# Moving output stores and transposes in the DMA queue of a fused sparse-attention and feed-forward kernel

## The chip, the cores and the metric

The kernel runs on one core of one Trainium2 chip. The metric is the device time of one execution in microseconds (us). The kernel before takes 322.76 us, the median of three runs (322.28, 322.76 and 325.9).

## What is computed

The reference first does attention over 8 batches of 8 heads with 576 positions of 64 numbers each. The first four heads are "local": a position sees itself and the 31 positions before it. The last four are "strided": a position sees those positions up to its own that have the same remainder modulo 32. The result, 4608 tokens of 512 numbers, goes through a bilinear feed-forward layer.

```python
scores = scale * np.matmul(q, k.transpose(0, 1, 3, 2))
scores = np.where(masks[None, :, :, :], scores, -1000000000.0)
attn = np.exp(scores - np.max(scores, axis=-1, keepdims=True))
attn = attn / (np.sum(attn, axis=-1, keepdims=True) + 1e-09)
x = np.matmul(attn, v).transpose(0, 2, 1, 3).reshape(B * S, H * D)
out = (x @ w_a) * (x @ w_b) @ w_out        # 512 -> 1536 -> 512
```

## The kernel before

**The feed-forward layer sets the beat.** The 4608 tokens are worked in nine passes t = 0 to 8 of 512 tokens. A pass has 16 slots, numbered 16t to 16t + 15. Slots 0 to 11 of a pass are its twelve groups of 128 hidden channels (`ffn_ab`): matrix products with w_a and w_b (TensorE, line 621), a copy of the first to SBUF by ScalarE (642), their product by VectorE (645) into `pf`. Slots 12 to 15 are the output product with w_out. In passes 1 to 8 this uses seven products of halves in place of eight (`y_plan`, matmuls at line 890), with sums made beforehand on VectorE (`fast_s`, line 824). Parts of the output are copied or added into two buffers `y_sb` of 512 KB each by `y_post` (ScalarE 855 and 861, VectorE 853, 857, 859), in the order 1, 7, 6, 4, 5, 2, 3. Parts 1 and 7 go to the first buffer, parts 6 and 5 to the second, so the third copy at line 855 is the first write to the second buffer. There are two buffers in all, and each pass uses both again. `store_half` sends one buffer to DRAM (store 0 and store 1, line 886).

**Attention is laid between these slots.** Batches are counted from 0 in the code, so the third batch is b = 2 and the fourth b = 3. A table names steps and their places: `STEPS` for batches 1 and 2, `LATER` for batches from 3 on, which run in pass b - 1. A whole number is the end of a slot; a half, such as 23.5, is the middle of the slot after it (24), between the two matrix products. The steps that matter here:

- `S0` to `S7`: scores of one unit (TensorE 378), exponential (ScalarE 398), mask (VectorE 416). S0 to S3 are local, S4 to S7 strided.
- `V0` to `V7`: the weighted sums. For local units TensorE (459), then a reciprocal (467) and a product (485) on VectorE into `xl`. For strided units TensorE (518), a logarithm and an exponential on ScalarE (525, 526; from pass 3 on 530, 531), a product on VectorE (527; 533) straight into `xT`.
- `O0`, `O1`: rows of the local heads from `xl` to a scratch in DRAM (`rows_out`, DMA of SyncE, line 500). `I0`, `I1`: back from it, transposed, into `xT` (`rows_in`, line 505), which the feed-forward layer reads.
- `Q0` to `Q3`: copies of transposed queries into zero-padded buffers `qz` (VectorE 334). Q0 and Q1 are local, Q2 and Q3 strided; S4 to S7 read what both Q2 and Q3 wrote.

**Loads and transposes.** `load_qk` lets POOL copy keys and queries of a batch into bf16 rows in DRAM (208 and 210, tensors `kr` and `qr`); `step_D` reads them back transposed through SyncE: line 321 for local keys and local queries, 324 for strided keys, 327 for strided queries in four pieces. The buffers are `kT` (two, by the batch's parity) and `qTl`, `qTs` (one each). `load_vl` (219) and `load_vs` (237) load values through POOL. Before a slot's POOL work a one-element copy (`pace`, 1138) makes POOL wait for that slot's result, so POOL's loads follow the passes.

**Order.** The instructions of each engine run in the order in which the program emits them. SyncE (SP) emits nothing but DMAs and their waits: stores, O, I and step_D all stand in its one queue, and one that waits holds those behind it. `do(i, fn)` puts a call at the end of slot i, behind the steps of the table with that number. For batches from 4 on step_D is placed in pass b - 2.

Of the kernel before, what the change touches and what calls it, by code (L numbers as in the profile page):

```python
# [32 lines left out]
def kernel(  # L33
# [531 lines left out]
    def F_mm(f, w, kk):  # L565
# [12 lines left out]
    STEPS = {1: {5.5: "Tk2", 6: "Tq2", 7: "S4 Tk3", 7.5: "S5", 8: "Tq3", 8.5: "V4", 9: "S6 V5 Pk0", 9.5: "S7 Pq0",  # L578
                 10: "V6 Tk0", 10.5: "Tq0 Pk1", 11: "Pq1", 12: "V7 Tk1 S0 W0 W1", 12.5: "Tq1 W2",
                 12.6: "S1", 12.75: "L0 X2", 13: "s2 X3 V0 m2 L1 W3", 13.5: "V1 S3", 14: "V2 X0", 14.5: "V3", 15: "X1"},  # L580
             2: {18: "Q0 Q1", 20: "S0", 20.5: "S1", 21: "V0", 21.5: "S2 Q2", 22: "V1 Q3", 22.5: "S3 O0", 23.5: "V2",
                 24: "S4 I0", 24.5: "V3 O1", 25: "S5", 25.5: "V4", 26: "S6", 26.5: "I1", 27: "V5", 27.5: "S7", ("y", 1, 6): "V6",
                 30: "V7"}}
    LATER = {-4: "Q0", -3: "Q1", -1: "S0", 0: "S1", 1: "V0", 2: "S2 Q2", 3: "V1 O0", 4: "S3 Q3", 5: "V2", 6: "S4", 7: "V3 O1 I0", 8: "S5", 9: "V4 I1",
             10: "S6",
# [13 lines left out]
    def take(pos):  # L599
        for b, names in steps.get(pos, ()):  # L600
            run(b, names)
# [5 lines left out]
    def mm_bank(shape):  # L607
        nm = "tp" if used[0] % 4 == 3 and used[0] >= 0 else "mm"
        used[0] += 1
        return psum4[nm].tile(shape, F32, tag=nm, name="mm")  # L610
# [218 lines left out]
    def products(t):  # L829
        pf, s = pfs[t], pss[t]  # L830
        full = lambda e, i: (lambda g, q: pf[:, 2 * g + e, HT * i + q:HT * (i + 1):2])
        summed = lambda n: (lambda g, q: s[:, n, g, q:HT:2])
        wsum = lambda n: (lambda g: wf[:, n, g])
        wfull = lambda e, j: (lambda g: wov[:, e, j, g])
        return {"1": ("X", full(0, 0), wfull(0, 0)), "2": ("Y", full(1, 0), wfull(1, 0)), "3": ("X", summed(3), wfull(1, 1)),
                "4": ("Z", full(1, 1), wsum(3)), "5": ("X", summed(0), wsum(0)), "6": ("X", summed(1), wsum(1)),
                "7": ("Z", summed(2), wsum(2))}
# [8 lines left out]
    def y_bufs():  # L846
        return [fsb.tile([128, 2, d_model], F32, tag="y_sb", name="y_sb", bufs=2) for _ in range(2)]

    def y_post(k, y, q, bank, n=slice(0, HN)):

        part = lambda i, j: y[i][:, q, HN * j:HN * (j + 1)]
        if k == "+":
            nc.vector.tensor_tensor(part(1, 1), part(1, 1), part(0, 1), op=ALU.add)  # L853
        elif k in "1765":
            nc.scalar.copy({"1": part(0, 0), "7": part(0, 1), "6": part(1, 0), "5": part(1, 1)}[k], bank)  # L855
        elif k == "4":
            nc.vector.tensor_tensor(part(1, 0), bank, part(1, 0), op=ALU.add)
        elif k == "2":
            nc.vector.tensor_tensor(y[0][:, q, n], bank, y[0][:, q, n], op=ALU.add)
        elif k == "3":  # L860
            nc.scalar.copy(part(0, 1), bank)
# [4 lines left out]
    def by_block(order, lead):  # L866

        head = order[:lead]
        return [(k, q, g) for k, q in head for g in range(FG - 1)] + [(k, q, FG - 1) for k, q in head] + [
            (k, q, g) for k, q in order[lead:] for g in range(FG)]  # L870

    def bank_of(nm, shape):
        return psum4[nm].tile(shape, F32, tag=nm, name="mm")

    def y_plan(t):

        plan, y = products(t), y_bufs()
        late = t in FAST_A
        if late:
            bank = {x: bank_of(nm, [128, 2, HN]) for x, nm in (("X", "mm"), ("Z", "mm"), ("Y", "tp"))}  # L880
        else:
            bank = {x: mm_bank([128, 2, HN]) for x in "ZXY"}

        def store_half(i):
            rows = out[TTOK * t:TTOK * (t + 1)].rearrange("(a i s q) c -> a s i (q c)", i=2, s=8, q=2)
            nc.sync.dma_start(out=rows[:, :, i], in_=y[i].rearrange("p q c -> p (q c)"))

        for k, q, g in by_block(Y_ORDER, 2 if late else 0):
            b, lhs, rhs = plan[k]
            nc.tensor.matmul(bank[b][:, q], lhsT=lhs(g, q), rhs=rhs(g), start=k in "172" and q == 0 and g == 0,  # L890
                             stop=g == FG - 1, skip_group_check=True)
            if g == FG - 1:
                if q == 1:
                    y_post(k, y, slice(0, 2), bank[b])
                    if k == "5":
                        y_post("+", y, slice(0, 2), None)
                take(("y", t, Y_ORDER.index((k, q)) + 1))
            yield y
        do(16 * t + 17, store_half, 0)
        do(16 * t + 18, store_half, 1)  # L900

    def y_tail(t):

# [30 lines left out]
    def ffn_ys(t, j, mid):  # L934
        if j == 0:
            yst[t] = (y_tail if t == NT - 1 else y_plan)(t)
        for i in range(21):
            y = next(yst[t])
            if i == 10:
                mid()  # L940
        if j == 3:
            for _ in yst[t]:
                pass
        return (y[0][:1, 0, :1], None, y[1][:1, 0, HN:HN + 1], y[1][:1, 0, :1])[j]
# [36 lines left out]
    with tc.manual_schedule(engines={ENG.PE, ENG.SP, ENG.Pool, ENG.DVE, ENG.Activation}):  # L981
# [26 lines left out]
        for nm in ORDER:  # L1008
            if nm[0] == "*":
                spin(int(nm[1:]))  # L1010
            elif nm in ("Ck", "Cq"):
                n = nm[1]
                x, cp = {"k": (raw[0], nc.vector.tensor_copy), "q": (raw[1], nc.scalar.copy)}[n]
                t = nats[0, n, False][:, 0:2].rearrange("p h r d -> p (h r d)")
# [54 lines left out]
        def do(i, fn, *args):  # L1069
            at.setdefault(i, []).append(lambda: fn(*args))  # L1070
# [11 lines left out]
        for b in range(FIRST_D, B):  # L1082
            g0 = 16 * (b - 2)
            if b == FIRST_D:
                do(0, load_qk, b, False)
                do(1, load_qk, b, True)
                do(14, load_vl, b)
                for h in range(HL):
                    do((16, 18, 19, 20)[h], load_vs, b, (h,))
            else:  # L1090
                do(19 if b == FIRST_D + 1 else g0 - 2, load_qk, b, False)
                do(21 if b == FIRST_D + 1 else g0 + 2, load_qk, b, True)
                for h in range(HL):
                    do(g0 + h + (15 if b == FIRST_D + 1 else 11), load_vs, b, (h,))
                do(g0 + (12 if b == FIRST_D + 1 else 9), load_vl, b)
            gs = {2: (13, 14, 15, 15), 3: (6, 6, 8, 14)}.get(b) or (3, 3, 4, 4)
            for (z, nm), g in zip(((0, "k"), (0, "q"), (1, "k"), (1, "q")), gs):
                do(g0 + g, step_D, b, z, nm)
        for n in range(4):
# [72 lines left out]
```

## Time and profile before

| What | Value |
|---|---|
| Median of the three runs | 322.76 us |
| The profiled execution's own time | 324.58 us |
| Its span, first to last instruction | 322.8 us |
| TensorE busy | 312.6 us |
| VectorE, ScalarE, POOL busy | 250.8, 192.9, 119.2 us |
| Granted TensorE clock | 0.999 |
| Stores of 512 KB by SyncE | 14 |
| Pass 1, pass 2 begin (TensorE) | 57.1, 91.0 us |
| Output products of passes 2, 3, 4, 5 begin | 117.3, 150.6, 184.0, 217.3 us |

Times in the profile are microseconds from the span's start. In a timeline a row gives start, duration, engine, line, operation, what it writes and what it reads, shapes, how many instructions were merged, and in square brackets the engine's idle time ahead of it and what ended that. For SyncE the duration is that of the issuing instruction; the time until the data has landed is told apart from it, in the answers on a line or a tensor. A list of waits gives who waited for whom: us in total, times, longest.

### The profile page before, as it was taken

To read this page: it belongs to the slowest core of one execution; us is meant where nothing else is said; L and a number is where in the kernel's file an instruction comes from. 1 tells how busy PE (TensorE), PEld (TensorE's weight loads), DVE (VectorE), ACT (ScalarE), POOL (GpSimd) and SP (SyncE) were. 2 spreads that over 40 slices of the span, in tenths; PEclk is the share of its full clock that TensorE was granted. 3 is DMA by queue.
4 is the path that set the end of the run, shared out by engine and by line. 5 is a ranking of instruction groups with operands and counts; after the bars stand their busy time and mean duration, and the time that the engine had idled before them with its cause. 6 is when DMAs were issued, how large, how long until landed. Compare 5 with 4: busy or idle time off the path is not lost.

```text
span 322.8 us, 7276 instructions
## 1 busy us (share of the span) xinstructions
PE 312.6 (97%) x2742; PEld 215.7 (67%) x2742; DVE 250.8 (78%) x574; ACT 192.9 (60%) x374; POOL 119.2 (37%) x211
## 2 busy tenths in 40 slices
PE   7999999999969999999999999999999999999994
PEld 5754565455945578656999996659655866786684
DVE  5877876588747988899689868997899667857862
ACT  6963776456744476558655775567656655535541
POOL 8845702781255143514550336133201012203520
PEclk9999999999999999999999999999999999999999
DMA  8999999999699999999999999989512040004004
GB/s 149 168 205 202 204 182 225 189 100 186 100 117 249 178 75 87 177 163 142 104 150 183 125 132 139 178 131 137 141 21 55 2 126 6 1 3 131 0 2 130
DMA packets 127059, 40.31 MB, mean 125 GB/s; under 512 B 114864, under 2 KB 124144, under 8 KB 126832
## 3 DMA queue, kind: packets, MB, share of 16 engines
q0 software_dynamic: 79760, 19.20, 63.6%
q1 hardware_dynamic: 47120, 20.59, 34.5%
q8 instruction: 21, 0.34, 0.5%
q14 instruction: 14, 0.11, 0.1%
q10 hardware_dynamic: 144, 0.07, 0.1%
HBM read 38.93 MB, written 18.28 MB: 177 GB/s over the span
## 4 chain that ended last, share of the span: by engine, by line
PE 90%; DMA 4%; DVE 3%; issue 1%; ACT 1%; POOL 0%; POOLq 0%
PE mm L621 36%; PE mm L890 17%; PE mm L770 6%; PE mm L706 4%; PE st L378 4%; PE mm L952 3%; PE ax L763 3%; PE o L459 3%; PE mm L763 2%; PE e L692 2%; DMA xT<-xd 2%; DMA shared<-in_q_dram 2%; PE mm L917 2%; PE mm L692 2%; PE end L917 1%; PE o L518 1%
## 5 line engine op out<-in xcount | busy, mean ns | idle before, releaser
L621 PE MATMUL mm<-xT,wa_sb 128*128 128x512 bf16 (+1 forms) x304 | 72.1, 356 | 2.6 <-DMA xT<-xd 2.6
L621 PE MATMUL mm<-xT,wb_sb 128*128 128x512 bf16 (+1 forms) x304 | 72.0, 357 | 0.0
L642 ACT COPY a_sb<-mm 128x512 f32<-128x512 f32 x68 | 39.8, 586 | 33.1 <-PE mm L621 31.4
L1138 POOL CAST pace<-pf 1x1 f32<-1x1 bf16 x71 | 20.8, 293 | 91.6 <-DVE pf L645 52.7
L645 DVE TENSOR_TENSOR pf<-a_sb,mm 128x512 bf16<-128x512 f32 x58 | 39.4, 679 | 12.2 <-ACT a_sb L642 8.6
L621 PEld LDWEIGHTS <-wb_sb 128*128 128x128 bf16 x304 | 29.2, 98 | 29.3 <-issue 2.9
L398 ACT ACTIVATE p<-st 72x576 bf16<-72x576 f32 (+1 forms) x56 | 36.4, 650 | 14.2 <-PE st L378 13.6
L621 PEld LDWEIGHTS <-wa_sb 128*128 128x128 bf16 x304 | 27.3, 98 | 17.4
L890 PEld LDWEIGHTS <-ps 128*128 128x128 bf16 x336 | 32.7, 98 | 3.7
L890 PE MATMUL mm<-wf,ps 128*128 128x256 bf16 x252 | 29.8, 273 | 0.0
L855 ACT COPY y_sb<-mm 128x512 f32<-128x512 f32 (+1 forms) x32 | 17.9, 559 | 19.1 <-PE mm L890 14.9
L1138 POOL COPY pace<-y_sb 1x1 f32<-1x1 f32 x22 | 9.7, 439 | 53.2 <-DVE y_sb L853 27.2
L770 PE MATMUL mm<-xT,wb_sb 128*128 128x512 bf16 x88 | 26.2, 379 | 0.0
L890 PEld LDWEIGHTS <-pf 128*128 128x128 bf16 x252 | 23.5, 98 | 2.7
L237 POOL DMA_DIRECT2D vs<-in_v_dram x24 | 21.8, 909 | 4.6 <-issue 3.1
L890 PE MATMUL mm<-wo_sb,pf 128*128 128x256 bf16 x168 | 21.8, 273 | 0.0
L824 DVE TENSOR_TENSOR ps<-pf 128x512 bf16<-128x512 bf16 (+1 forms) x49 | 19.6, 400 | 0.8
L706 PE MATMUL mm<-xT,wb_sb 128*128 128x512 bf16 (+1 forms) x80 | 19.1, 336 | 0.0
L416 DVE TENSOR_TENSOR p<-p,mask_l 128x576 int16<-128x576 int16 x32 | 14.5, 454 | 5.8 <-ACT p L398 5.5
L533 DVE TENSOR_TENSOR xT<-o,xr 64x288 bf16<-64x288 f32 x16 | 7.7, 480 | 13.5 <-ACT xr L531 13.4
L459 PEld LDWEIGHTS <-p 128*128 128x128 bf16 (+1 forms) x256 | 13.1, 97 | 6.2 <-DVE xr L485 1.0
L416 DVE TENSOR_TENSOR p<-p,mask_s 72x576 int16<-72x576 int16 x28 | 12.6, 451 | 1.9 <-ACT p L398 1.7
(211 smaller groups left out, 639.4 us busy)
## 6 DMA issues: line engine op xcount, KB each, us to landing
out_dram<-y_sb SPq DMA_DIRECT2D x14, 512.0 KB, 5.1
kr<-in_k_dram POOLq DMA_DIRECT2D x12, 288.0 KB, 8.5
qr<-in_q_dram POOLq DMA_DIRECT2D x12, 288.0 KB, 9.3
vl<-in_v_dram POOLq DMA_DIRECT2D x6, 384.0 KB, 7.2
out_dram<-y_sb SPq DMA_DIRECT2D x7, 256.0 KB, 3.3
vs<-in_v_dram POOLq DMA_DIRECT2D x24, 72.0 KB, 4.9
xd<-xl SPq DMA_DIRECT2D x12, 144.0 KB, 4.3
wo_sb<-in_moe_w_out_dram POOLq DMA_DIRECT2D x4, 384.0 KB, 11.3
```

The costliest lines, as they stand in the source:

```text
L237: nc.gpsimd.dma_start(out=vs_buf[b % 2][:, h, :, 0:D], in_=v[b, HL + h].rearrange("(p r) d -> p r d", r=RS))
L398: nc.scalar.activation(p_flat(p)[:M, :2 * W].rearrange("p (i n) -> p i n", n=2 * n), st[:M].rearrange("p a (i n) -> p (a i) n", n=256)[:, ...
L416: nc.vector.tensor_tensor(pi, pi, mk, op=ALU.bitwise_and)
L459: nc.tensor.matmul(of[:, j, i, :w], lhsT=pt, rhs=vt, start=True, stop=True)
L621: nc.tensor.matmul(ps_[:, c0:c0 + n], lhsT=w[:, kk, 128 * f:128 * (f + 1)], rhs=xT[:, kk, x0:x0 + n], start=(kk == first and c0 == 0), sto ...
L642: nc.scalar.copy(a_sb, ab[0])
L645: nc.vector.tensor_mul(pf[:, f, :].rearrange("p (i a s) -> p a i s", i=2, s=16), halves(a_sb), halves(ab[1]))
L706: nc.tensor.matmul(dst, lhsT=wb_sb[:, kk, 128 * f:128 * (f + 1)], rhs=rhs, start=kk == 0 and k in (None, 0), stop=kk == KD - 1 and k in (N ...
L770: nc.tensor.matmul(got[e], lhsT=wb_sb[:, kk, 128 * f:128 * (f + 1)], rhs=xT[:, kk, x0:x0 + TTOK], start=kk == 0, stop=kk == KD - 1)
L824: nc.vector.tensor_tensor(s[:, n], a, b, op=op)
L890: nc.tensor.matmul(bank[b][:, q], lhsT=lhs(g, q), rhs=rhs(g), start=k in "172" and q == 0 and g == 0, stop=g == FG - 1, skip_group_check=True)
L1138: nc.gpsimd.tensor_copy(pace, done)
```

## The change

Three things move; no operation is added or taken away, but for POOL's one-element pace copies, which stand only in slots that have such a call.

1. In pass 1, the table of batch 2 (the third batch): V2 goes from the middle of slot 24 to the end of slot 23, S4 from the end of slot 24 to its middle, V3 and O1 from the middle of slot 25 to the end of slot 24, S5 from the end of slot 25 to its middle. I0 stays at the end of slot 24, now ahead of O1. Q3 goes from the end of slot 22 to the end of slot 23.
2. Batch 3 (the fourth batch): the transpose of its strided keys goes from slot 24 to slot 30, that of its strided queries from slot 30 to slot 31. For batches 4 to 7 the transpose of the local keys goes from group 3 to group 2 of its pass, ahead of O0.
3. The two stores of a pass go from groups 1 and 2 of the next pass to groups 3 and 7. In group 3 store 0 stands behind O0 and the local queries' transpose; in group 7 store 1 stands behind O1 and I0.

```diff
-             2: {18: "Q0 Q1", 20: "S0", 20.5: "S1", 21: "V0", 21.5: "S2 Q2", 22: "V1 Q3", 22.5: "S3 O0", 23.5: "V2",
-                 24: "S4 I0", 24.5: "V3 O1", 25: "S5", 25.5: "V4", 26: "S6", 26.5: "I1", 27: "V5", 27.5: "S7", ("y", 1, 6): "V6",
+             2: {18: "Q0 Q1", 20: "S0", 20.5: "S1", 21: "V0", 21.5: "S2 Q2", 22: "V1", 22.5: "S3 O0", 23: "V2 Q3",
+                 23.5: "S4", 24: "V3 I0 O1", 24.5: "S5", 25.5: "V4", 26: "S6", 26.5: "I1", 27: "V5", 27.5: "S7", ("y", 1, 6): "V6",
                  30: "V7"}}
...
-        do(16 * t + 17, store_half, 0)
-        do(16 * t + 18, store_half, 1)
+        do(16 * t + 19, store_half, 0)
+        do(16 * t + 23, store_half, 1)
...
-            gs = {2: (13, 14, 15, 15), 3: (6, 6, 8, 14)}.get(b) or (3, 3, 4, 4)
+            gs = {2: (13, 14, 15, 15), 3: (6, 6, 14, 15)}.get(b) or (2, 3, 4, 4)
             for (z, nm), g in zip(((0, "k"), (0, "q"), (1, "k"), (1, "q")), gs):
                 do(g0 + g, step_D, b, z, nm)
```

The SyncE queue of pass 4, as an example, in the new order: local keys (321), O0, local queries (321), store 0, strided keys (324), strided queries (327, four), O1, I0, store 1, I1. In the old order: store 0, store 1, O0, local keys, local queries, strided keys, strided queries, O1, I0, I1.

## The prediction

> **What bounds the kernel now.** First the page's busy times and clock: TensorE works 97% of the span at full clock. Then the waits, those of TensorE alone: after the start-up only one is worth anything.
>
> ```profile
> PE 312.6 (97%) x2742; PEld 215.7 (67%) x2742; DVE 250.8 (78%) x574; ACT 192.9 (60%) x374; POOL 119.2 (37%) x211
> PEclk9999999999999999999999999999999999999999
> ...
> PE mm L621 <- DMA xT<-xd: 2.6, 1, 2.6
> ```
>
> So no edit to queues can win more than those 2.64 us, 0.8% of the span, and any new wait of TensorE adds in full, since it has no other idle time to absorb it. The chain that ended last shows where the wait comes from, at the turn from pass 1 to pass 2:
>
> ```profile
> 85.48 3.62 DMA xd<-xl
> 89.11 5.54 DMA xT<-xd
> 94.69 1.02 PE mm L621 x4
> ```
>
> Rows of the third batch go out to DRAM (O1, 85.48), come back transposed (I1, 89.11), and TensorE, ready at 94.69 - 2.64 = 92.05, starts at 94.69. Next the timeline of SyncE, which issues one after the other:
>
> ```profile
> 78.44 0.53 SPq L500 DMA_DIRECT2D xd<-xl  x1
> 82.82 1.16 SPq L505 DMA_TRANSPOSE xT<-xd  x1
> 84.08 1.31 SPq L324 DMA_TRANSPOSE kT1s<-kr  x1
> 85.48 0.53 SPq L500 DMA_DIRECT2D xd<-xl  x1
> ```
>
> O1 stands behind the fourth batch's strided key transpose (L324). Its data was done long before: the last xl of VectorE (L485) runs 76.67 to 77.22.
>
> **Part 1: pass 1, third and fourth batch.** The L324 transpose leaves this place, so O1 follows I0 at 84.1, 1.4 us sooner. It landed 3.6 us after its issue, behind L324; with a quiet queue (237.8, 245.3) 2.2 to 2.7. I take 2.9: landed at 87.0, where I1 is issued. I1 took 5.5 us beside a load of vl (issued 84.51, landing 7.7 us later), I0 at 82.82 without one 2.6: it lands at 89.6 to 92.5, against 94.7.
>
> The same edit puts Q3 (L334, a copy into qz) one group later, to the end of group 7 (slot 23), and its reader S4 (TensorE, L378) half a slot sooner, to the middle of slot 24. VectorE runs behind TensorE there:
>
> ```profile
> 72.32 0.46 DVE L334 COPY qz0s<-qTs 64x1152 bf16<-64x1152 bf16 x1
> 72.81 0.43 DVE L824 TENSOR_TENSOR ps<-ps,pf 128x512 bf16<-128x512 bf16 x1
> 73.16 0.45 DVE L416 TENSOR_TENSOR p<-p,mask_l 128x576 int16<-128x576 int16 x1
> 73.52 0.68 DVE L645 TENSOR_TENSOR pf<-a_sb,mm 128x512 bf16<-128x512 f32 x1
> ...
> 73.02 0.35 PE L459 MATMUL o<-vl,p 128*128 128x65 bf16 x6
> 74.06 0.41 PE L378 MATMUL st<-qz0s,kT0s 128*128 128x144 bf16 x4
> ```
>
> VectorE's new order is L824, mask, pf, then V2's reciprocal (0.18) and product (0.55), then Q3 (0.46). Without Q3 at 72.32 pf ends near 73.6; plus 0.18, 0.55, 0.46 and gaps, Q3 ends at 74.85. S4's turn comes where V2 stood, 73.02, plus 0.35 for V2 now ahead of it and its wait for V1's product (72.29): 73.35. TensorE waits some **1.5 us**; behind S4 stand the second half of group 8, V3, S5 and ScalarE's exponential, on which VectorE's mask waits in turn, so all of pass 1 goes 1.6 us later. At worst S4 waits for the whole DVE lag, 2.6; at best (VectorE taking its work in the gaps) nothing. TensorE then wants its rows at 92.05 + 1.6 = 93.65; I1, even with vl shifted the same 1.6, has landed. Gain: 94.69 - 93.65 = **1.0 us**, between 0 and 2.64.
>
> Fourth batch's transposes: the four of queries (L327, 5.86 us of SyncE, from 90.33) now follow I1 and L324: 87.0 + 1.1 + 1.3 = 89.5, no later than before. Their first reader is VectorE's copy at 100.94, just after they land (100.8); its reader S4 runs at 107.20. Cost 0; if they came 3 us late, S4 has six to spare. It is the strided keys' first reader as well.
>
> **Part 2: passes 2 to 5, the stores.** In SyncE's queue store 0 moves behind the local query transpose, store 1 behind O1 and I0, the local key transpose ahead of O0. What changes is when store 1 lands, because its buffer (y_sb, two buffers) is written again by the same pass's third output copy on ScalarE (L855). This timeline row shows that the copy does wait for SyncE's DMAs:
>
> ```profile
> 154.99 0.59 ACT L855 COPY y_sb<-mm 128x512 f32<-128x512 f32 x1 [0.77 <-DMA qTs<-qr]
> ```
>
> The releaser named shares its semaphore with the old store, landed at 137.4; there TensorE ended that idle time. Behind the copy TensorE accumulates into the bank that it reads (156.32 in pass 3): slack 156.32 - 155.58 = 0.7; through V6's logarithm, exponential and product to V7 about 0.5. Every further us is one of TensorE.
>
> Store 1's issue, from pass 4's rows:
>
> ```profile
> 171.09 0.33 SPq L500 DMA_DIRECT2D xd<-xl  x1
> 171.70 2.78 SPq L321 DMA_TRANSPOSE kT0l<-kr  x1
> 174.68 2.88 SPq L321 DMA_TRANSPOSE qTl<-qr  x1
> 177.66 1.30 SPq L324 DMA_TRANSPOSE kT0s<-kr  x1
> 179.06 5.90 SPq L327 DMA_TRANSPOSE qTs<-qr  x4
> 185.05 0.53 SPq L500 DMA_DIRECT2D xd<-xl  x1
> 185.63 4.84 SPq L505 DMA_TRANSPOSE xT<-xd  x2
> ```
>
> O0 waits for V1 and stays. After it: L321 of queries 2.9, store 0 0.6, L324 1.3, four L327 5.0 to 5.9, O1 0.5, I0 1.2, gaps 0.5: 12.0 to 12.9 us. Store 1 is issued at 183.5 to 184.4; from the O0 of passes 2, 3, 5 (103.17, 137.77, 204.51) likewise 115.5, 150.2, 216.9 at the earliest. A store of 512 KB landed 4.1 us after issue where nothing else ran (261.8), 4.6 to 5.9 as first of a pair beside loads, 6.4 to 9.1 as second. The copies start at 121.7, 155.0, 188.5, 221.7.
> - Lower bound: 4.1 gives landings at 119.6, 154.3, 187.6, 221.0, all in time: cost 0. It can't go below that, since TensorE waits for no load or store in these passes now.
> - Upper bound: landings on this queue come in the order of issue, so store 1 lands behind I0. I0 landed at 123.6, 158.2, 190.9, 224.0 (5.9, 5.0, 5.3, 5.2 after issue), held up by the vl load (L219, at 114.7, 148.2, 181.6, 215.2, landing 6.5 to 7.4 later). If I0 does not come sooner, store 1 adds the 0.6 to 1.25 by which the second of a quiet pair lands behind the first: waits of up to 3.1, 4.4, 3.7, 3.5, less four slacks of 0.5: 12.7.
> - Between: 6.0 us, just over the first stores of the busy pairs. Landings 121.5, 156.2, 189.5, 222.9; waits 0, 1.2, 1.0, 1.2, less slack: **1.9 us**. I take this, because SyncE issues the transposes 1 to 2 us sooner and more of them are through before vl's packets come.
>
> One row decides how far to trust that: the last L327 of pass 4, issued 183.7, lands 5.4 us later, 189.1, just after vl (181.6 + 7.1 = 188.7). SyncE's transposes starve while POOL's load runs. The Trainium skill, "DMA: Bandwidth & Descriptors", section "Queues, rings and completion order", says that each engine takes turns between the queue rows that have work, packet by packet. By that, store 1 would get its turn beside vl; the row speaks against it for transposes, and no run here shows it for 4 KB pieces.
>
> The key transpose ahead of O0 delays O0 only if its rows are late. They landed 10.4 to 10.6 us after issue beside the stores (128.3, 161.2, 194.7), 5.6 and 6.6 without (66.6, 90.5). At 6.6 L321 is over by 137.4, 170.7, 204.1, just ahead of O0: cost 0; at 10.4 O0 and store 1 come 3 us later and the upper bound holds. I1 in pass 3 landed at 160.7 against a need at 161.64: SyncE's lead of 1 to 2 us covers the store now ahead of it. One pace copy less per pass on POOL (63% idle): 0.
>
> **Passes 6 to 8:** 0. In pass 6 store 1 follows I0 at 247, eight us before its copy (255.0); later passes hold no transposes.
>
> **Sum:** -1.0 + 1.9 = **+0.9 us**, on the profiled execution's own 324.58 (span 322.8 and 1.8 around it) 325.5. The median of the runs shown, 322.76, lies 1.8 below that execution: **323.7**. A measurement tells about 1% (3.2 us) from no change.
>
> **Rivals and chances.**
> - Forecast, some of both: 322.3 to 326, 0.38.
> - Store 1 gets its turn beside vl and lands in time; only part 1 counts: 322.76 - 1.0 = 321.8. For: lone stores take 4.1. Against: five transposes stand ahead of it. This is the outcome by that rule of the Trainium skill. 0.20.
> - No wait for Q3 either: 322.76 - 2.64 = 320.1. For it VectorE must not lag; its rows show 1.4 us. 0.07.
> - Slower: store 1 waits behind I0 and vl. With I0 1.2 us sooner and the store 1.2 behind it, it lands at 123.6, 158.2, 190.9, 224.0: waits 1.9, 3.2, 2.4, 2.3, less 2.4 of slack, 7.4; minus 1.0 gives **329.2**. It decides from landings of some 6.8 us on. For: the starved L327. 0.30.
> - The change misses its aim: I1 falls into the shifted vl load, the row wait stays beside the new ones: 322.76 + 1.9 = 324.7. 0.05.
>
> Range: 320.0 to 330.0 takes in all but the ends. Faster by over 1% (under 319.5) needs more than the one wait holds: 0.04. Slower by over 1% (over 326.0): the fourth case, 0.30. Within: 0.66.
>
> **What would show it.** TensorE's wait for xT gone; a wait of TensorE or its weight load for VectorE at S4 of 1 to 2 us near 73; O1 right behind I0. In passes 2 to 5, ScalarE's idle time ahead of the third L855 over 0.8 and ended by a DMA, TensorE waiting for ScalarE right after. I am wrong if these copies start on time and S4 too (then 320), or if key rows still take 10 us (then near 330).

## The result, and the profile after

The changed kernel is slower. Its median is 338.23 us of five runs (335.73 to 341.62), that of the kernel before 324.62 us of five (322.28 to 329.33; the three runs told above and two more). The ratio is 1.0415, with a 95% interval of 1.0317 to 1.0513; it leaves out single disturbed executions, and so it is not just the quotient of the medians. The forecast was 323.7 us with a range up to 330.0: both are missed, on the slow side.

The profiled execution after took 335.73 us, its span is 334.0 us, 11.2 us above the span before (322.8). First the page's busy times and clock, as before the change:

```profile
PE 315.3 (94%) x2714; PEld 217.7 (65%) x2742; DVE 251.8 (75%) x574; ACT 192.9 (58%) x374; POOL 117.4 (35%) x207
PEclk9999999999999999999999979999899999999999
```

TensorE is busy for 2.7 us more than before, with the same work (28 of its 2742 products are missing from this trace), and two slices of its clock row are no longer full. Next, TensorE's waits (in total, times, longest):

```profile
PE mm L890 <- ACT y_sb L855: 8.2, 4, 2.3
PE st L378 <- DVE qz0s L334: 1.3, 1, 1.3
```

The wait for `xT` is gone. Four waits of the output products for ScalarE's third copy have come in its place, one in each of the passes 2 to 5, and one wait of S4 for Q3's copy. ScalarE's own list says what that copy waits for:

```profile
ACT y_sb L855 <- DMA out_dram<-y_sb: 14.7, 4, 4.0
```

That is store 1, all four times: the copy starts 0.1 us after store 1 has landed in each of these passes. In pass 4 the timeline shows the chain. ScalarE is idle for 3.96 us ahead of the copy (0.77 us before the change), and TensorE for 2.33 us ahead of its next products in that bank.

```profile
194.48 0.59 ACT L855 COPY y_sb<-mm 128x512 f32<-128x512 f32 x1 [3.96 <-DMA out_dram<-y_sb]
195.12 2.02 PE L890 MATMUL mm<-wf,ps 128*128 128x256 bf16 x12 [2.33 <-ACT y_sb L855]
```

After two of the four waits TensorE goes on at half speed for a while. The answer on windows gives, for each stretch, its length, TensorE's busy time with the number of instructions, the granted clock, the share of the DMA engines (above 1 where transfers queue, since one counts in the stretch in which it starts) and GB/s:

```profile
192.00:195.90 3.90, 1.57 (x16) 1.00 1.31 204
195.90:199.30 3.40, 3.40 (x24) 0.50 0.07 7
199.30:202.70 3.40, 3.35 (x26) 1.00 0.38 27
233.40:236.80 3.40, 3.40 (x24) 0.50 0.04 8
```

The two half-speed stretches last 3.41 us each and do 1.7 us of work, so each costs 1.7 us.

Where the 11.2 us of the span are, stage by stage (us from one stage's first product to the next's):

| Stage | Before | After | Difference |
|---|---|---|---|
| Start-up | 22.4 | 21.4 | -1.0 |
| Pass 0 and the channel groups of pass 1 | 58.4 | 60.0 | +1.6 |
| Pass 2, channel groups | 26.3 | 23.9 | -2.4 |
| Output products of passes 2, 3, 4, 5 | 10.2 each | 12.4, 12.6, 14.3, 14.0 | +12.5 |
| All the rest | | | +0.5 |

The 12.5 us of the output products are the four waits (1.80, 2.01, 2.33, 2.02: 8.2), the two half-speed stretches (3.4), and some 0.9 that is left, most of it in passes 2 and 3, where V7 starts 0.4 us later than the wait alone makes it. The start-up differs between executions of one kernel: in three executions of the kernel before, the output products of pass 1 begin at 79.7, 80.0 and 80.8 us.

### The profile page after: what moved, and what is told of

The parts are those of the page before. It is cut to its first block, busy times and chain, and to the rows that moved or that the text cites. A ratio compares the mean times of both kernels' runs of the same rounds, so it can differ in the third digit from the quotient of the medians.

```text
span 334.0 us, 7236 instructions
## 1 busy us (share of the span) xinstructions
PE 315.3 (94%) x2714; PEld 217.7 (65%) x2742; DVE 251.8 (75%) x574; ACT 192.9 (58%) x374; POOL 117.4 (35%) x207
## 5 line engine op out<-in xcount | busy, mean ns | idle before, releaser
L621 PE MATMUL mm<-xT,wa_sb 128*128 128x512 bf16 (+1 forms) x287 | 70.3, 355 | 0.6
L1138 POOL CAST pace<-pf 1x1 f32<-1x1 bf16 x68 | 19.6, 288 | 91.1 <-DVE pf L645 44.3
L890 PE MATMUL mm<-wf,ps 128*128 128x256 bf16 x252 | 30.5, 276 | 8.2 <-ACT y_sb L855 8.2
L890 PEld LDWEIGHTS <-pf 128*128 128x128 bf16 x252 | 24.6, 102 | 3.6
L770 PE MATMUL mm<-xT,wb_sb 128*128 128x512 bf16 x83 | 25.2, 379 | 0.1
L890 PE MATMUL mm<-wo_sb,pf 128*128 128x256 bf16 x168 | 24.1, 291 | 0.0
L416 DVE TENSOR_TENSOR p<-p,mask_l 128x576 int16<-128x576 int16 x32 | 14.5, 454 | 6.4 <-ACT p L398 6.0
L459 PEld LDWEIGHTS <-p 128*128 128x128 bf16 (+1 forms) x256 | 13.2, 97 | 6.7 <-DVE xr L485 1.0
L416 DVE TENSOR_TENSOR p<-p,mask_s 72x576 int16<-72x576 int16 x28 | 12.6, 451 | 2.7 <-ACT p L398 2.5
```

The source lines that it names most:

```text
L416: nc.vector.tensor_tensor(pi, pi, mk, op=ALU.bitwise_and)
L621: nc.tensor.matmul(ps_[:, c0:c0 + n], lhsT=w[:, kk, 128 * f:128 * (f + 1)], rhs=xT[:, kk, x0:x0 + n], start=(kk == first and c0 == 0), sto ...
L770: nc.tensor.matmul(got[e], lhsT=wb_sb[:, kk, 128 * f:128 * (f + 1)], rhs=xT[:, kk, x0:x0 + TTOK], start=kk == 0, stop=kk == KD - 1)
L1138: nc.gpsimd.tensor_copy(pace, done)
```

## The experiments

The questions were: which of the parts costs the time; whether store 1 is late because SyncE issues it late (store 0 now stands ahead of the strided key transpose) or because its landing is held by POOL's `vl` load (theory C in the expectations); and what part 1 is worth alone. Each ratio is against the kernel before on the same chip.

**The two stores alone.** Edit to the kernel before:

```diff
-        do(16 * t + 17, store_half, 0)
-        do(16 * t + 18, store_half, 1)
+        do(16 * t + 19, store_half, 0)
+        do(16 * t + 23, store_half, 1)
```

> The two stores alone in groups 3 and 7; everything else as before. Theory A: the third output copy waits in passes 2 to 5 as in the changed kernel (ScalarE idle 3 to 4 us ahead of it, TensorE 2 us each); 8 to 13 us slower than before, and the wait for xT stays. Rival (it takes the key transpose ahead of O0 as well, which pushes all of SyncE's queue back): under 5 us slower.

Measured: 341.72 us, ratio 1.0580 (1.0520 to 1.0639). It is the whole loss and more: some 19 us where 8 to 13 were expected, with the expected waits, but three of them twice as long. TensorE's waits for the third copy are 4.75, 2.02, 4.04 and 3.78 us, and the clock row shows three slow places:

```profile
PE mm L890 <- ACT y_sb L855: 14.6, 4, 4.7
PE mm L621 <- DMA xT<-xd: 0.7, 1, 0.7
...
PEclk9999999999999978999999989999899999999999
```

So the other moves of the change make the stores cheaper, not dearer.

**The changed kernel with its stores back.** Edit to the changed kernel: the same four lines the other way.

> The changed kernel with both stores back in groups 1 and 2: part 1 and the key transposes in group 2 remain. If the stores are the whole loss, it is like the part 1 kernel: within 1% of before, no wait of the third copy, the S4 wait of 1.3 us. If the key transpose ahead of O0 costs something of its own, it is 1% or more slower than before and TensorE shows a wait other than S4's.

Measured: 322.88 us (10 runs), ratio 1.0017 (0.9984 to 1.0051), no wait for the third copy. With the run above this settles the first question: the stores are the loss.

**Store 1 alone.** Edit to the kernel before: only `16 * t + 18` to `16 * t + 23` for store 1.

> The kernel before with store 1 alone moved, to group 7. If store 1's place behind O1 and I0 is enough, the third copy waits in passes 2 to 5 here too, TensorE 1.5 us or more each, and this kernel is 7 us or more slower than before. If it takes both stores, the waits are under 0.7 us and the time is within 3 us of before.

Measured: 334.32 us, ratio 1.0352 (1.0280 to 1.0425); waits of 1.61, 1.56, 1.75 and 2.29 us, and one half-speed stretch behind the last. As the first case expected, store 1 in group 7 is enough for most of the loss, with store 0 left where it was.

**Store 0 back in group 1.** Edit to the changed kernel:

```diff
-        do(16 * t + 19, store_half, 0)
+        do(16 * t + 17, store_half, 0)
```

> The changed kernel with store 0 back in group 1 and store 1 left in group 7. If store 0 among the transposes is what makes SyncE's strided key transpose take 2.7 to 3.5 us in place of 1.3 to 2.6, store 1 is issued 1.5 to 2.5 us sooner after O0 (12.5 to 13.5 us in place of 14.5 to 15.3) and TensorE's waits fall to 0 to 0.8 us each: 6 to 12 us under the changed kernel. If the number of transposes in flight sets it, the waits stay at 1.5 us or more.

Measured: 332.93 us, ratio 1.0287 (1.0229 to 1.0345). SyncE's timeline of pass 4, first of the changed kernel, then of this one:

```profile
173.97 2.12 SPq L500 DMA_DIRECT2D xd<-xl  x1
176.19 1.56 SPq L321 DMA_TRANSPOSE qTl<-qr  x1
177.85 0.58 SPq L886 DMA_DIRECT2D out_dram<-y_sb  x1
178.52 3.00 SPq L324 DMA_TRANSPOSE kT0s<-kr  x1
181.62 5.68 SPq L327 DMA_TRANSPOSE qTs<-qr  x4
187.39 0.53 SPq L500 DMA_DIRECT2D xd<-xl  x1
187.97 1.25 SPq L505 DMA_TRANSPOSE xT<-xd  x1
189.27 0.59 SPq L886 DMA_DIRECT2D out_dram<-y_sb  x1
```

```profile
177.91 1.49 SPq L324 DMA_TRANSPOSE kT0s<-kr  x1
179.51 5.80 SPq L327 DMA_TRANSPOSE qTs<-qr  x4
185.41 0.53 SPq L500 DMA_DIRECT2D xd<-xl  x1
185.99 1.28 SPq L505 DMA_TRANSPOSE xT<-xd  x1
187.31 0.60 SPq L886 DMA_DIRECT2D out_dram<-y_sb  x1
```

The strided key transpose takes SyncE 1.25 to 1.99 us in the four passes here, 2.73 to 3.50 with store 0 just ahead of it. But the waits hardly change, where the first case expected 0 to 0.8 us, and there is no half-speed stretch:

```profile
PE mm L890 <- ACT y_sb L855: 7.9, 4, 2.2
```

Counted from the first output product of its pass, store 1 is now issued 0.4 to 1.4 us behind it (before this edit 1.0 to 2.6), and lands 7.0 to 7.35 us behind it (7.0 to 7.5). A store that is issued sooner and lands at the same time must be held by something else; the next two runs ask whether that is the `vl` load.

**Without the vl load.** Batches 4 to 7 get no `vl` load, first in the changed kernel:

```diff
-                do(g0 + (12 if b == FIRST_D + 1 else 9), load_vl, b)
+                if b == FIRST_D + 1:
+                    do(g0 + 12, load_vl, b)
```

> The changed kernel with the load of local values (line 219) left out for batches 4 to 7, whose local heads then use the values of older batches; nothing else is left out. Theory C (O1, I0 and store 1 stand still while POOL's load of vl runs and land only behind it, 4.3 to 5.1 us after the output products begin): without it O1 and I0 land 2.5 to 4 us after their issue, store 1 some 4.1 to 4.7 after its own, that is 5.2 to 7 us after the output products begin in place of 7.0 to 7.5; TensorE's waits fall from 8.2 us in all to 2 to 4. Rival (SyncE's late issue of store 1 alone): landing 4.6 to 5.9 us after issue as before, waits unchanged.

Measured in a single execution: 340.94 us. The waits are 0.16, 4.43, 1.81 and 4.97 us, 11.4 in all, where theory C expected 2 to 4. O1 landed 2.6 to 3.0 us after its issue, as it expected, and so did I0 in three of the four passes (2.7 to 3.6); store 1 took 4.5 to 5.8 us, where 4.1 to 4.7 were expected. But store 1 was issued late: 3.8 and 5.1 us behind the first output product in passes 3 and 5, where the local queries' transpose took 5.2 and 6.1 us of SyncE, and 1.9 us in pass 4. In pass 4 it then landed 7.0 us behind that product, with no `vl` load running. So a late issue makes TensorE wait without the load too. To take away both, the load was also left out with store 0 in group 1:

> Store 0 back in group 1, and the load of local values left out for batches 4 to 7 as in the run beside this one. Store 0 alone had changed the issue of store 1 (0.4 to 1.4 us after the output products begin in place of 1.0 to 2.6) but not its landing (7.0 to 7.4). Theory C: with both gone it lands 4.5 to 5.8 us after they begin, TensorE's four waits are under 0.7 us each, and the time is 7 to 11 us under that of the store 0 kernel. Rival: the waits stay near 1.9 us each.

Measured: 325.30 us, ratio 1.0062 (1.0000 to 1.0124), against 1.0287 with the load.

```profile
PE mm L890 <- ACT y_sb L855: 1.6, 2, 1.2
```

Store 1 lands 4.6 to 6.4 us behind the first output product (7.0 to 7.35 with the load) and 4.5 to 4.8 us after its issue (5.8 to 6.6 with it). Pass 3 missed theory C's limits, with a landing at 6.4 us and a wait of 1.17; the gain of 7.6 us against the store 0 kernel is as it said. So in this kernel, where SyncE issues store 1 early enough, the load is what holds it; by what means, no run here tells.

In the changed kernel both causes count, for taking away one alone leaves the waits: 7.9 us with the earlier issue, 11.4 without the load. Store 1 landed there 5.93, 4.65, 5.11 and 5.51 us after its issue. Set against the 4.5 to 4.8 without the load, the load's own share is, as an estimate, some 1.3, 0, 0.4 and 0.9 us in passes 2 to 5; the rest of the lateness is the late issue. The order of the landings fits theory C: O1, I0 and store 1 come down one by one right behind `vl`. In passes 2 to 5 `vl` landed at 120.46, 155.26, 191.27 and 229.40, O1 at 120.55, 155.72, 191.90 and 229.57, I0 at 120.98, 156.57, 192.56 and 230.03, store 1 at 122.50, 158.15, 194.38 and 231.48.

**Store 1 ahead of O1 and I0.** In the changed kernel store 1 goes to group 5 (`16 * t + 21`).

> The changed kernel with store 1 two groups sooner, in group 5: behind the four strided query transposes, but ahead of O1 and I0. Theory A (the copy waits for the landing of store 1): it is issued 1.8 us sooner, with two transfers fewer ahead of it, and lands 2 to 3 us sooner; TensorE's four waits of 1.8 to 2.3 us shrink to 0 to 0.5, the half-speed stretches go with them, and the time is 8 to 12 us under the changed kernel's. Rival (O1, I0 and the strided transposes are late as such): the waits stay.

Measured: 335.92 us, ratio 1.0313 (1.0228 to 1.0399). The expectation missed. The profiled execution is the longest of the four (338.79 us), so the sizes of its waits (0.98, 2.36, 5.45 and 1.75 us) need not hold for the others. In it store 1 still took 5.2 to 7.2 us to land, and the local queries' transpose held SyncE for 5.9 and 7.6 us in passes 3 and 4. In passes 2 and 5 store 1 was issued 0.6 and 0.2 us ahead of the first output product, and yet landed 1.2 to 1.3 us behind `vl` (123.83 behind 122.55, 235.87 behind 234.65). Being ahead of O1 and I0 did not help there.

**Both stores in group 3.** In the changed kernel store 1 goes to `16 * t + 19`, right behind store 0.

> The changed kernel with store 1 in group 3 too, right behind store 0: ahead of the strided transposes, O1 and I0 instead of behind them, some 9 us earlier in the queue. Theory A: store 1 lands well before the third copy, the four waits go, and the time is that of the part 1 kernel, 1 to 2 us under before. Rival (stores in the middle of the transposes cost as such, by delaying rows that TensorE needs): still over 4 us slower than before, with waits of TensorE for xT or qz.

Measured: 330.19 us, ratio 1.0120 (1.0049 to 1.0190), with executions from 326.06 to 336.02. In the profiled one (326.06) no copy waits for a store, and all that shows beside S4's wait is a half-speed stretch in the start-up. Once more:

> The changed kernel with both stores in group 3, a second look. If its executions differ, this one shows waits of TensorE in passes 2 to 5 or more half-speed stretches, which the first had not; if they don't, it has the S4 wait alone and a span near 324 us again.

Measured: 326.40 us. Again no copy waits for a store, but TensorE waits for rows at the turn to pass 4:

```profile
PE mm L621 <- DMA xT<-xd: 2.1, 2, 1.1
```

With both stores ahead of O1 and I0 the loss can thus move to the rows. Whether that accounts for all of the 1.2% stays open, since the two profiled executions differ.

**The key transpose back in group 3.** In the changed kernel `(2, 3, 4, 4)` becomes `(3, 3, 4, 4)`.

> The changed kernel with the local key transpose back in group 3, behind O0; stores as in the change. If the key transpose ahead of O0 spares SyncE its 2.5 to 3 us between O0 and store 1, its return makes store 1 later by about as much and TensorE's waits grow from some 2 us each to 3.5 to 5, as in the stores-alone kernel: 5 to 10 us slower than the changed kernel. If it rather delays O0 and so costs something, this kernel is the faster one.

Measured: 342.69 us, ratio 1.0609 (1.0549 to 1.0669), waits of 3.02, 3.80, 4.37 and 1.41 us. In passes 2 to 4 the waits grew, though to 3.0 to 4.4 us and not quite the 3.5 to 5 of the first case; in pass 5 they did not. So the key transpose ahead of O0 is worth some 2% in this kernel: behind O0 it takes 2.8 us of SyncE in pass 4, and from O0 to the issue of store 1 it is 17.2 us (179.39 to 196.55) in place of 15.3.

**Part 1 alone.** The kernel before with the new table of batch 2 and the new places of the fourth batch's transposes:

> Part 1 alone: pass 1's new table and the fourth batch's transposes later; stores and local key transposes as before. Theory A (the loss is the third output copy waiting for store 1, part 1 is a small gain): TensorE's wait for xT (2.64 us) goes, its wait for Q3's copy at S4 (1.3 us in the changed kernel) stays, so some 1.3 us faster than before; no wait of ScalarE's third copy for a DMA, no half-speed clock. Theory B (part 1 itself costs: pass 1 gets longer by more than the wait that goes): within 0.5 us of before or slower.

Measured: 324.02 us (12 runs), ratio 1.0042 (1.0004 to 1.0081). Theory A's gain of 1.3 us did not come: part 1 is no gain, as theory B said. The rest of theory A came. The wait for `xT` is gone, S4's wait has come, and no third copy waits for a store:

```profile
PE st L378 <- DVE qz0s L334: 1.3, 1, 1.3
```

**Part 1 with Q3 where it was.** Edit to the kernel just told of:

```diff
-             2: {18: "Q0 Q1", ..., 22: "V1", 22.5: "S3 O0", 23: "V2 Q3",
+             2: {18: "Q0 Q1", ..., 22: "V1 Q3", 22.5: "S3 O0", 23: "V2",
```

> As the part 1 kernel, but with Q3's copy back at the end of slot 22, a slot ahead of S4. If the S4 wait comes from the copy's new place, it goes and nothing is late in its stead: TensorE has no wait over 0.5 us after the start, the whole 2.64 us are won against before, 1.3 us against the part 1 kernel. If VectorE's lag alone sets S4, a wait of about 1 us stays and the two part 1 kernels are alike.

Measured: 321.70 us (12 runs), ratio 0.9992 (0.9960 to 1.0024). The copy is done in time and S4 follows it without a wait:

```profile
71.47 0.46 DVE L334 COPY qz0s<-qTs 64x1152 bf16<-64x1152 bf16 x1
...
72.56 0.41 PE L378 MATMUL st<-qz0s,kT0s 128*128 128x144 bf16 x4
```

Its largest later wait of TensorE is 0.27 us. So S4's wait came from the copy's new place. But the 2.64 us were not won: this kernel, the fastest found, cannot be told from the kernel before. That asks what the wait for `xT` was worth.

**The kernel before, twice more.**

> The kernel before, once more, for a second look at its wait for xT at the turn to pass 2 (2.64 us in the first profile, 0.67 in the stores-alone kernel, whose pass 1 is the same). If the wait is a standing cost, it is 2 us or more again; if it is a matter of the single execution, it lies anywhere from 0 to 2.6.

> The kernel before, a third look at the same wait, with the same two expectations.

Measured: 322.14 and 321.93 us, spans 320.4 and 320.2, and the one wait is 1.43 and 0.86 us in them, not 2.64:

```profile
PE mm L621 <- DMA xT<-xd: 1.4, 1, 1.4
```

```profile
PE mm L621 <- DMA xT<-xd: 0.9, 1, 0.9
```

The two kernels that kept this part of the order had 0.67 (stores alone) and 1.45 us (store 1 alone).

## Why the prediction was wrong

**What was right.** The path was as told. The wait for `xT` went, S4 waits for Q3's copy, in passes 2 to 5 ScalarE's third copy waits for a DMA and TensorE for that copy, and the change is slower. The sizes were not: part 2, forecast at 1.9 us of TensorE's waits, measured 8.2, and 12.5 with what came behind them.

**What failed: the term "12.0 to 12.9 us" from O0 to store 1, and with it "Between: 6.0 us, just over the first stores of the busy pairs".** O0 stayed where it was (in pass 4, 12.95 us ahead of the first output product before and 12.89 after). From its start, with O0's own 0.33 us, the forecast had 12.3 to 13.2 us to the issue of store 1; measured are 15.2, 15.3, 15.3 and 14.5. Store 1 was to be issued 1.8 to 0.4 us ahead of the first output product (in pass 4 at 183.5 at the earliest, with the product at 184.0); it was issued 1.0, 2.5, 2.4 and 1.7 us behind it.

The reason given was that "SyncE issues the transposes 1 to 2 us sooner and more of them are through before vl's packets come". The strided key transpose was indeed sooner, by 1.6 to 2.7 us against the first output product. But it lasts 2.73 to 3.50 us in place of "L324 1.3", and most of the lead is spent on it: the four strided queries' transposes begin 0.2 us later in pass 2, 0.3 sooner in pass 4, and 1.4 and 1.9 sooner in passes 3 and 5. O0 itself holds SyncE for 1.57 and 2.12 us in passes 3 and 4, in place of 0.33. The 1.3 was read from pass 4 alone; passes 3 and 5 before the change already had more:

```profile
144.76 2.59 SPq L324 DMA_TRANSPOSE kT1s<-kr  x1
210.71 2.30 SPq L324 DMA_TRANSPOSE kT1s<-kr  x1
```

With that the two events that I wanted apart fall together: the landings on SyncE's queue, store 1 last, and the end of the `vl` load.

The landing time itself was not too low: 5.9, 4.65, 5.1 and 5.5 us after issue, under my 6.0. But it is no constant to add to an issue. The experiment with store 0 in group 1 gave part of the issue back and kept the landing; without `vl` as well, the landing came 0.8 to 2.6 us sooner, pass by pass. What held was the sentence of the **upper bound**, "landings on this queue come in the order of issue, so store 1 lands behind I0", and the row that I had shown against my own choice, the starved L327 of pass 4. The outcome by the round-robin rule of the Trainium skill ("DMA: Bandwidth & Descriptors", section "Queues, rings and completion order"), priced as the second rival, did not come: store 1, with its 4 KB pieces, came down 1.5 to 1.8 us behind I0, and I0 behind `vl`, in all four passes.

**The fourth rival came closest.** Store 1 does land behind I0 and `vl`, and the rival's waits less slack came to 7.4 us; measured are 8.2. It did not name the late issue, which by the estimate above makes up the larger part of the delay in passes 3 and 4. Its slack was right: in pass 4 the copy was 3.2 us later, counted from the first output product, than in the kernel before (7.62 against 4.43 us), and TensorE waited 2.33; that leaves 0.9, near the 0.7 read from the reuse of the bank. Its chance, 0.30, was too small for a mechanism that had a row of the trace on its side and only a lead of "1 to 2 us" against it. The range ended at 330.0, although the prediction's own upper bound of 12.7 us makes it 334.5.

**What no case held: the clock.** "Any new wait of TensorE adds in full" was too little. Two of the four waits were followed by 3.41 us at half speed, 3.4 us in all in the profiled execution. With them the fourth rival's 329.2 would have been 332.6. The profiled execution, the fastest of the five, took 335.73; the other four took 338.04 to 341.62 at a granted clock of 0.975 to 0.985, against its 0.987. They left no profile, so the way to the median of 338.23 is not accounted for term by term.

**Part 1 (gain 1.0 us) did not come.** In the two profiled executions the stages up to the end of pass 2's channel groups are 0.8 us shorter together, apart from the start-up, near the forecast. Its steps were right one by one: S4's wait for Q3 measured 1.33 us against 1.5, O1 right behind I0, the wait for `xT` gone. In the changed kernel:

```profile
73.30 0.46 DVE L334 COPY qz0s<-qTs 64x1152 bf16<-64x1152 bf16 x1
...
73.90 0.41 PE L378 MATMUL st<-qz0s,kT0s 128*128 128x144 bf16 x4 [1.33 <-DVE qz0s L334]
...
81.42 1.16 SPq L505 DMA_TRANSPOSE xT<-xd  x1
82.67 0.63 SPq L500 DMA_DIRECT2D xd<-xl  x1
```

The mis-sized term is the 2.64 us that goes: the first profile showed a long example of a wait that was 0.67, 0.86, 1.43 and 1.45 us in the other four executions seen, 1.1 on their mean. Trading 1.1 for 1.33 is a loss of some 0.2 us, 0.1%, at the low end of the +0.4% (0.04 to 0.81%) that part 1 alone measured; what the rest of it is stays open.

**Right as told:** the key rows landed 5.7 to 6.0 us after issue in passes 3 to 5 (the prediction puts the cost at 0 for 6.6), so that the transpose ahead of O0 did not delay its start; the fourth batch's transposes cost next to nothing (a wait of 0.29 us for `vl`, at 95.75 us); passes 6 to 8 are unchanged but for 0.4 us.

## What to carry to other kernels

The place of a store in a queue is not priced by its own transfer time: count everything on the queue from the last point that you know, each instruction at its longest among the passes and with its new neighbours (here 2.7 to 3.5 us for a transpose put at 1.3), and then ask which load of another queue is running when it is to land. If the trace has one row where transfers of this queue stand still behind that load, price that row's outcome first. Two causes can each be enough: here neither the earlier issue nor the missing load alone removed the waits, and only both together did for the most part. A wait of the bounding engine seen in one profiled execution is a sample: profile a second execution before counting its removal as a gain, and count for each new wait of some 2 us that the clock may drop behind it.

## What the runs showed of the hardware

**A wait of about 2 us can halve TensorE's clock afterwards.** The half-speed stretches last 3.41 us or twice that, and their starts in one execution lie on a grid of 3.413 us (195.88 and 233.43 in the changed kernel: 11 steps). What decides is TensorE's idle time inside one step of that grid. Worked out from the waits and the grid, 2.02 and 2.33 us (the changed kernel), 2.24 us (store 1 alone), 2.40, 3.18 and 3.41 us (stores alone), 2.55 and 3.38 us (key transpose in group 3) were followed by a slow step. 1.80 us (the changed kernel), 1.98 us (store 0 in group 1) and 2.01 us (stores alone) were not, so the limit lies near 2 us in these traces. A wait of 3.02 us that the grid cut into 1.66 and 1.36 brought none. A second slow step followed where TensorE was idle for 0.85 us or more within the first (1.57 us in the stores-alone kernel, 1.25 and 0.98 with the key transpose in group 3, 0.85 and 2.75 without the `vl` load), and none where that was 0 to 0.32. The Trainium skill, "TensorE: Matmul & The Clock Gate", section "What's actually happening", gives the free-running window of 3413 ns, and the grid agrees; it puts the half-speed state behind at least one idle window, and here the measurement differs: some 2 us of the 3.41 are enough.

**SyncE's time for one and the same transpose varies.** In passes 2 to 5 the strided key transpose held SyncE for 2.73 to 3.50 us in the changed kernel, with a 512 KB store just ahead of it, and for 1.25 to 1.99 us with that store in group 1. A store ahead is not the only way to a long time: the kernel before had 2.59 and 2.30 us in passes 3 and 5, and 2.97 us in pass 3 of a further execution, with none there. What else sets it stays open.
